# Fourier mixing and MLP on one core: the residual x added by accumulating DMAs, and the split of z done two quarters at a time

## The chip, the core and the metric

The kernel runs on one NeuronCore of one Trainium2 chip. A core has five engines that each follow a list of instructions in order: PE (matrix multiplication into PSUM), DVE (vector), ACT (scalar and activation functions), POOL (GpSimd) and SP. They wait for each other through semaphores. DMAs move data between DRAM and the on-chip memory SBUF; here SP and POOL issue nearly all of them, and each issue stands in its engine's list, in order, together with the wait in front of it. The metric is the device time of one execution in microseconds; the lower the better.

## The reference

With x of 2048 rows (the sequence) by 1024 columns (hidden), C and S the cosine and sine matrices of the discrete Fourier transform, and six rows `sa, ca, ga, sb, cb, gb` that are made from a conditioning vector `c`:

```python
h = _layernorm(x, axis=-1) * (1 + ca) + sa
a = jnp.einsum("bsd,ed->bse", h, dft_hid_re)
b = jnp.einsum("bsd,ed->bse", h, dft_hid_im)
y = jnp.einsum("ts,bse->bte", dft_seq_re, a) - jnp.einsum("ts,bse->bte", dft_seq_im, b)
x = x + ga * y
h = _layernorm(x, axis=-1) * (1 + cb) + sb
z = _layernorm(h, axis=-1)
x = x + gb * (gelu(z @ w1 + b1) @ w2 + b2)
```

All arrays are float32; w1 is 1024 x 3584 and w2 is 3584 x 1024. The change concerns the line `x = x + ga * y`, the mean in the layer norm behind it, and the preparation of `z` for the product with w1.

## The kernel before

The function `fast` computes everything under the assumption that the four Fourier matrices have the usual symmetries; it checks them on the way, and only if they don't hold does a second function, `general`, run. Only `fast` is changed.

**Stages.** First, up to about 215 us of the profile, x is loaded in 16 tiles of 128 rows, normalised (`ln1`, four tiles at a time), transposed, folded with the help of the symmetries, and transformed along the hidden dimension (`hid_unit`). Then comes the stage of the change, a loop over eight blocks `b` of two tiles each (L3171): `seq_tile` does the transform along the sequence for a tile (P and Q on PE) and evacuates it to SBUF as y with two DVE instructions (L3044, L3049); `ln2` forms x1 = x + ga * y, its layer norm with cb and sb, and the layer norm after that; `turn` transposes the result on PE and ACT copies it to a buffer `zt` (L3140); `z_tasks` splits it. Last come 28 groups of the product with w1 (`gemm3`, L3523) interleaved with 14 of the product with w2 (`gemm4`, L3632). The groups 0 to 12 of the first product use the first four blocks, which stay in SBUF; the z of blocks 4 to 7 is stored to DRAM by POOL (L3161) and loaded for the rest.

**The split of z.** The large products use seven products of half-size quarters in place of eight, and each float32 operand is a pair of float16 arrays, a high and a low part. `z_tasks` therefore takes the four quarters of a block (512 columns each), forms four differences on DVE in place (L2392, `comb`), and makes seven operands: the high part by ACT (L2367, `hi`) and the low part by DVE (L2377, `lo`).

**ln2 before.** For each tile n of a block: y = y * ga (L3104), y = y + x with the sum of each row kept (L3105), and a store of the tile, which is x1, to the output by POOL (L3107). x comes by `load_xw`, one DMA of 1 MB a block on SP's queue (L3066), into the block's work buffer `w`. Then: minus the mean (L3108), squares with their sum on ACT (L3088), (y - mean) * cb into w (L3113), a square root on ACT and a reciprocal refined on DVE (L2612 to L2621), times that and plus sb (L3117), the squares again with y as scratch (L3088), a second root, and the final scaling on ACT (L3126). Buffers y and w exist for three blocks.

**What sets the order.** Instructions are first collected as tasks with an engine, a cost, dependencies and a due time, in streams. A planner (`pick_first`, `fill_to`) takes the task of the least due time that can start at once, or the one that starts soonest, and thereby fixes each engine's list. Its clock is a model; it never sees the chip. The model counts a lag `LAT = 0.15` behind each dependency, 0.3 (`BEHIND`) ahead of a store, and a time to land:

```python
LANDS = {"dma": 2.0, "st": 4.0, ("st", "d"): 7.0, ("st", "u"): 5.0, ("st", "s"): 4.0, ("st", "z"): 4.0}
```

A task of kind "st" (made by `store`) is emitted, in POOL's or SP's list, as soon as the task that it depends on has been emitted. `flush` (L3391) ends this stage's planning; everything ahead of it precedes the first product on each engine. Behind it, POOL adds a row to the output by 16 DMAs that accumulate in DRAM (L3806), and later by others of that kind (L3730, L3705).

## Time and profile before

| | us |
|---|---|
| median of 3 runs | 1451.27 |
| lowest, highest run | 1444.45, 1453.93 |
| the execution that was profiled | 1453.19 |
| its span, first to last instruction | 1451.4 |
| first gated tile (L3104), start | 216.4 |
| last gated tile (L3104), start | 360.4 |
| time of one accumulating DMA's issue on POOL (L3806, median) | 0.868 |
| time of one plain store's issue on POOL (L3107, median) | 0.534 |

The profile is of one execution. Busy times of engines overlap; the mean duration of an instruction in a row is somewhat longer than the distance between two starts, because an engine begins the next instruction before the last one has drained. "x14" is a count; "out<-in" names the buffers, where `arena` is the one large SBUF buffer that nearly everything lives in, `ps` is PSUM, `fzc` the stored z, and `out_dram` the output. "idle ... <-X" is time in which the engine stood still until X released it. An engine name with q (SPq, POOLq) is its queue of issues and waits. A DMA's time to landing runs from its issue to its completion.

### The profile page before, as it was taken

How to read it: one execution, taken by the hardware profiler on the slowest of the kernel's cores; microseconds unless marked ns; L12 is line 12 of the kernel's file. 1: busy time of each engine (PE TensorE's matmuls, PEld its weight loads, DVE VectorE, ACT ScalarE, POOL GpSimd, SP SyncE). 2: the span in 40 equal slices, each digit the busy share in tenths (PEclk: the TensorE clock that was granted, in tenths of full speed). 3: DMA queues.
4: the chain of work that ended last, by engine and by line, in shares of the span. 5: the costliest groups of instructions: out<-in, count | busy, mean ns of one | idle time of the engine just before them, and what ended most of it. 6: DMA issues, size and time to landing. Idle time of an engine off the chain costs nothing.

```text
span 1451.4 us, 17321 instructions
## 1 busy us (share of the span) xinstructions
PE 1309.9 (90%) x6050; PEld 624.2 (43%) x6050; DVE 1105.7 (76%) x1668; ACT 749.5 (52%) x1209; POOL 260.3 (18%) x427
## 2 busy tenths in 40 slices
PE   5798979864487999999999999979999999999988
PEld 2344436543233444444444444434444444444433
DVE  5886738999657798989898898645666667777786
ACT  5486226787755683737373534145535353535340
POOL 3000000002420000000000000244443433353401
PEclk9798979986698999999999999999999999999999
DMA  9981442228698362626362539698877787876735
GB/s 371 369 317 45 131 130 102 87 103 292 226 202 272 115 226 95 225 95 225 109 225 95 202 111 368 178 323 278 294 247 233 249 292 244 288 249 241 233 125 119
DMA packets 108057, 302.29 MB, mean 208 GB/s; under 512 B 13836, under 2 KB 13852, under 8 KB 106040
## 3 DMA queue, kind: packets, MB, share of 16 engines
q1 hardware_dynamic: 74712, 192.49, 38.0%
q0 software_dynamic: 33216, 108.60, 23.7%
q8 instruction: 49, 0.80, 0.2%
q14 instruction: 48, 0.39, 0.1%
q10 hardware_dynamic: 32, 0.01, 0.0%
HBM read 216.10 MB, written 84.93 MB: 207 GB/s over the span
## 4 chain that ended last, share of the span: by engine, by line
PE 66%; issue 3%; DMA 2%; POOL 1%; DVE 1%; ACT 1%; POOLq 0%; ACTq 0%; DVEq 0%
PE ps L3632 35%; PE ps L3523 31%; DMA arena<-in_cre_dram 1%; DMA arena<-in_w_dram 1%; POOL fzc L3161 1%; DVE arena L2379 1%; POOL out_dram L3806 0%; ACT arena L2367 0%; POOL out_dram L3730 0%; DVE arena L2392 0%; POOL arena L3454 0%; DVE arena L3549 0%; ACT arena L3088 0%; ACT arena L3545 0%; ACT arena L3428 0%
## 5 line engine op out<-in xcount | busy, mean ns | idle before, releaser
L3523 PE MATMUL ps<-arena 128*128 128x512 f16 x2352 | 521.3, 384 | 25.5 <-ACT arena L3545 20.3
L3632 PE MATMUL ps<-arena 128*128 128x512 f16 x2352 | 512.6, 380 | 4.5 <-ACT arena L3668 4.5
L3523 PEld LDWEIGHTS <-arena 128*128 128x128 f16 x2352 | 232.5, 99 | 311.9 <-issue 41.3
L3632 PEld LDWEIGHTS <-arena 128*128 128x128 f16 x2352 | 230.8, 98 | 284.1 <-issue 8.1
L3678 DVE SCALAR_TENSOR_TENSOR arena<-ps,i4c,arena 128x1024 f32<-128x1024 f32 x179 | 229.4, 1282 | 99.9 <-PE ps L3632 96.7
L2392 DVE TENSOR_TENSOR arena<-arena 128x512 f32<-128x512 f32 (+1 forms) x228 | 171.4, 753 | 5.4 <-ACT arena L3140 1.1
L2367 ACT ACTIVATE arena<-arena,shc 128x512 f16<-128x512 f32 (+1 forms) x115 | 115.9, 1016 | 112.2 <-DVE arena L2392 62.6
L2379 DVE SCALAR_TENSOR_TENSOR arena<-arena,shc 128x512 f16<-128x512 f32 (+1 forms) x115 | 128.8, 1122 | 39.0 <-ACT arena L2367 38.8
L3428 ACT ACTIVATE arena<-arena 128x512 f32<-128x512 f32 (+5 forms) x148 | 91.1, 617 | 122.2 <-DVE arena L3437 119.0
L3542 ACT ACTIVATE arena<-arena,b1s,i1c 128x512 f32<-128x512 f32 x84 | 68.2, 814 | 118.8 <-DVE arena L3549 118.6
L3549 DVE TENSOR_TENSOR arena<-arena,ps 128x512 f32<-128x512 f32 x84 | 57.4, 685 | 61.1 <-PE ps L3523 60.5
L3437 DVE TENSOR_TENSOR arena<-arena 128x256 f32<-128x256 f32 x240 | 88.7, 419 | 16.9 <-DMA arena<-in_cre_dram 16.9
L2367 ACT ACTIVATE arena<-arena,s1c 128x512 f16<-128x512 f32 (+1 forms) x70 | 60.5, 886 | 71.2 <-DVE arena L2392 51.3
L3237 POOL PARTITION_ALL_REDUCE sums<-sums x21 | 12.7, 607 | 412.8 <-DVE sums L3233 408.1
L3454 POOL DMA_DIRECT2D arena<-in_cim_dram x99 | 53.6, 544 | 114.4 <-ACT arena L3428 105.2
L2379 DVE SCALAR_TENSOR_TENSOR arena<-arena,s1c 128x512 f16<-128x512 f32 (+1 forms) x70 | 66.3, 958 | 9.5 <-ACT arena L2367 9.4
L3545 ACT ACTIVATE arena<-ps 128x512 f32<-128x512 f32 x84 | 49.4, 589 | 38.8 <-PE ps L3523 38.8
L3454 POOL DMA_DIRECT2D arena<-in_cre_dram x99 | 54.2, 548 | 79.8 <-ACT arena L3428 62.7
L3225 ACT ACTIVATE ps<-arena 128x1024 f32<-128x1024 f32 x52 | 53.0, 1019 | 27.1 <-DMA arena<-in_w_dram 12.3
L2953 PE MATMUL ps<-arena 128*128 128x257 f16 (+5 forms) x297 | 54.2, 342 | 13.1 <-DVE arena L2518 8.3
L2885 PE MATMUL ps<-arena,scol 128*128 128x512 f32 x128 | 60.0, 618 | 3.4 <-DMA arena<-in_wm_dram 2.2
L2379 DVE SCALAR_TENSOR_TENSOR arena<-arena,s2c 128x1024 f16<-128x1024 f32 x49 | 61.9, 1279 | 1.4 <-ACT arena L2367 1.3
(198 smaller groups left out, 1217.6 us busy)
## 6 DMA issues: line engine op xcount, KB each, us to landing
fw<-arena SPq DMA_DIRECT2D x73, 512.0 KB, 5.7
arena<-fw SPq DMA_DIRECT2D x112, 256.0 KB, 4.7
arena<-fw SPq DMA_DIRECT2D x49, 512.0 KB, 4.6
arena<-in_cre_dram POOLq DMA_DIRECT2D x96, 256.0 KB, 4.7
arena<-in_cim_dram POOLq DMA_DIRECT2D x96, 256.0 KB, 5.2
out_dram<-arena POOLq DMA_DIRECT2D x44, 512.0 KB, 6.9
arena<-in_wm_dram SPq DMA_DIRECT2D x32, 512.0 KB, 7.3
arena<-in_w_dram SPq DMA_DIRECT2D x56, 256.0 KB, 3.7
```

The costliest lines, as they stand in the source:

```text
L2367: act.activation(o[m][0], q(j), AF.Copy, **sc)
L2379: dve.scalar_tensor_tensor(o[m][1], q(j), scale, o[m][0], op0=ALU.mult, op1=ALU.subtract)
L2392: dve.tensor_tensor(q(d), q(a), q(b), op=op)
L2885: pe.matmul(bank(6 + h), scol[:, k : k + 1].to_broadcast([P, P]), FA(o + 512 * h, (1, 512)), start=k == 0, stop=k == 7,)
L3428: f = lambda: act.activation(sq(a), sq(a), AF.Square, accum_out=csum[0:pn, n : n + 1])
L3437: dve.tensor_tensor(a[:, o::2], a[:, o::2], b[:, o::2], op=op)
L3454: return lambda t: gp.dma_start(t[0:pn], v)
L3523: pe.matmul(ps.rearrange("p (k t) -> p k t", k=4), w1c[:, m, s, a, d * P : (d + 1) * P], zc(m)[:, b, :, d, :], start=(start and d == 0 and ...
L3542: act.activation(dst, src, AF.Gelu_apprx_tanh, scale=inv, bias=b1s[:, 2 * p + j : 2 * p + j + 1])
L3549: after_pe("dve", 0.6, lambda: dve.tensor_tensor(q, q, ps[b], op=ALU.add), kp[b])
L3632: pe.matmul(t[:, j], hidc[:, c_, m, a, k * P : (k + 1) * P], w2c[:, m, c_, w], start=(start and c_ == 0 and n == 0), stop=(c_ == 1 and n = ...
L3678: lambda: dve.scalar_tensor_tensor(dst, ps[b], inv, dst, op0=ALU.mult, op1=ALU.add), kp[b],
```

## The change

- `load_xw` and its eight loads are removed. In `ln2` one DVE instruction per tile multiplies y by ga and keeps the sum of each row; then POOL issues a DMA that reads x from DRAM and adds it to y in SBUF (`accum_op=ALU.add`); the store of x1 waits for that DMA's landing, and so does the square of the tile (`("st", "xa", i)`). The squares, which write `w` first now, also take over the dependencies that `load_xw` had for the reuse of `w` (`wfree`).
- The sum no longer contains x. Its mean is kept from `ln1`: the small buffers `mvs` give way to columns of `csum`, which has an early use now, and where ACT makes the statistics (tiles 12 to 15) it scales so that the column is the mean itself. Minus the mean of x1 is then -sum/D minus the kept mean.
- `z_tasks` is written out instead of calling `right_tasks`. The high and the low parts take two quarters (1024 elements) in one instruction for the operands (0, 1), (3, 4), (2, 5), with 6 alone; of the differences the first two are one instruction, the others stay single. Each step has its dependencies written out.
- The planner counts no lag where a DVE or ACT task depends on one of its own engine (`by`). This holds for the whole of `fast`.

```diff
@@ class Task @@
-                    t = max(t, done.get(d, 1e12) + self.lag)
+                    t = max(t, done.get(d, 1e12) + (0.0 if by.get(d) == self.eng else self.lag))
...
         def run(self):
             t = self.start() + self.cost
+            if self.eng in ("dve", "act"):
+                by[self.key] = self.eng
@@ ln1 @@
-        mv, lc = mvs[bt % 2], lncs[bt % 2]
+        mv, lc = csum[:, 8 * bt : 8 * bt + 8].rearrange("p (q k) -> p q k", k=2), lncs[bt % 2]
...
-                act.activation(junk, FA(xr(i), (1, 1024)), AF.Copy, accum_out=mv[:, q, 0:1])
+                act.activation(junk, FA(xr(i), (1, 1024)), AF.Copy, scale=1.0 / D, accum_out=mv[:, q, 0:1])
...
-        scale, mean = (0.25, -1.0) if bt < ACT_STATS else (0.25 / D**3, -1.0 / D)
+        scale = 0.25 if bt < ACT_STATS else 0.25 / D
@@ ln2 @@
-    def load_xw(b):
-        f = lambda: sp.dma_start(wb(b), x_s[b // 4, 2 * b % 8 : 2 * b % 8 + 2].rearrange("r p e -> p r e"))
-        deps = [("turn", 2 * b - 6 + n) for n in range(2)] if b > 2 else [*copk, ("gbst", 0), ("gbst", 1)] if b > 1 else hops
-        load(("xw", b), f, deps, cost=2.8, stream="xw", due=70.0)
...
-        last[0] = ("xw", b)
+        wfree = [("turn", 2 * b - 6 + n) for n in range(2)] if b > 2 else [*copk, ("gbst", 0), ("gbst", 1)] if b > 1 else hops
         for n in range(2):
             i = 2 * b + n
-            step("dve", 1.23, lambda n=n: dve.tensor_tensor(y[:, n], y[:, n], ga_t, op=ALU.mult), [("y", i), *rows])
-            step("dve", 1.28, lambda n=n: dve.scalar_tensor_tensor(
-                y[:, n], y[:, n], 1.0, w[:, n], op0=ALU.mult, op1=ALU.add, accum_out=su[:, n : n + 1]), key=("x1", i))
-            store("x1", i, lambda n=n, i=i: gp.dma_start(o_s[i // 8, i % 8], y[:, n]), ("x1", i))
-        step("dve", 0.17, lambda: dve.tensor_scalar(nm, su, -1.0 / D, None, op0=ALU.mult))
+            last[0] = None
+            k = step("dve", 1.32, lambda n=n: dve.scalar_tensor_tensor(
+                y[:, n], y[:, n], 1.0, ga_t, op0=ALU.mult, op1=ALU.mult, accum_out=su[:, n : n + 1]), [("y", i), *rows])
+            store("xa", i, lambda n=n, i=i: gp.dma_start(y[:, n], x_s[i // 8, i % 8], accum_op=ALU.add), k)
+            store("x1", i, lambda n=n, i=i: gp.dma_start(o_s[i // 8, i % 8], y[:, n]), ("st", "xa", i))
+        step("dve", 0.17, lambda: dve.scalar_tensor_tensor(
+            nm, su, -1.0 / D, csum[:, 4 * b : 4 * b + 4 : 2], op0=ALU.mult, op1=ALU.subtract))
         q = sq(y, w, 1.0, nm)
         for n in range(2):
-            step("act", 1.35, q(n))
+            step("act", 1.35, q(n), [("st", "xa", 2 * b + n), *wfree])
@@ z_tasks @@
-        return right_tasks(
-            q, outs, None, 512, lambda j: ("zt", 2 * b + j % 2), lambda m: ("z", b, m), post=post if h else None,
-            free=(lambda m: slot("z", lambda: (b - 1, n[0]))) if h else None,
-        )
+        def hi(ms, js, deps):
+            def f():
...
+                act.activation(places(ms, 0), q(*js), AF.Copy)
...
+            add("z", "act", 0.17 + 0.44 * len(ms), f, deps + free, (b, "zhi", ms), due, f"z{b}")
+            return (b, "zhi", ms)
+
+        def lo(ms, js, deps):
+            def f():
+                dve.tensor_tensor(places(ms, 1), q(*js), places(ms, 0), op=ALU.subtract)
...
+            t = add("z", "dve", 0.13 + 0.54 * len(ms), f, deps, (b, "zlo", ms), due, f"z{b}")
+            return t
+
+        def comb(d, a, c, deps, key):
+            f = lambda: dve.tensor_tensor(q(*d), q(*a), q(*c), op=ALU.subtract)
+            return add("z", "dve", 0.15 + 0.54 * len(d), f, deps, (b, "zc", key), due, f"z{b}")
+
+        due = 110.0 + 22.0 * b
+        order = (0, 1, 3, 4, 2, 5, 6)
+        src = [("zt", 2 * b), ("zt", 2 * b + 1)]
+        k0 = lo((0, 1), (0, 2), [hi((0, 1), (0, 2), src[:1])])
+        k1 = comb((0, 1), (1, 3), (0, 1), [k0, *src], 0)
+        h1 = hi((3, 4), (0, 1), [k1])
+        k2 = lo((3, 4), (0, 1), [h1])
+        k3 = comb((1,), (3,), (0,), [k2], 1)
+        h2 = hi((2, 5), (1, 3), [k3])
+        k4 = comb((2,), (2,), (1,), [k3], 2)
+        k5 = lo((2, 5), (1, 3), [h2])
+        lo((6,), (2,), [hi((6,), (2,), [k4])])
@@ the loop over blocks @@
     for b in range(NB):
-        load_xw(b)
         for n in range(2):
             seq_tile(2 * b + n)
         ln2(b)
         for n in range(2):
             turn(2 * b + n)
-        push("z", f"z{b}", z_tasks(b), 110.0 + 22.0 * b)
+        z_tasks(b)
```

More of the change, by code (lines that the diff above doesn't have):

```diff
@@ L2598, in fast @@
     add("modm", "dve", 0.8, cols_out, ["cols", "max"], "mod", 1.0)
-    mvs = [mk([P, 4, 2], F32, f"mv{n}") for n in range(2)]
+    csum = mk([P, 160], F32, "csum")
     lncs = [mk([P, 4, 4], F32, f"lnc{n}") for n in range(2)]
@@ L3159, in post, with q @@
-        def post(m, o_):
-            dst = zc_d[m][:, :, k].rearrange("p a c t -> p a (c t)")
-            store("z", (b, at_[m]), lambda: gp.dma_start(dst, o_[2]), ("z", b, m), f"z{b}")
-        return right_tasks(
-            q, outs, None, 512, lambda j: ("zt", 2 * b + j % 2), lambda m: ("z", b, m), post=post if h else None,
-            free=(lambda m: slot("z", lambda: (b - 1, n[0]))) if h else None,
-        )
+        made = []
+        def q(i, j=None):
+            o = [ZT0 + 1024 * (n % 2) + 512 * (n // 2) for n in (i, i if j is None else j)]
+            return FA(o[0], (o[1] - o[0], 2), (1, 512)) if j is not None else FA(o[0], (1, 512))
@@ new lines, in places @@
+        def places(ms, a):
+            if h == 0:
+                o = [512 * O_ZC[m] + 2048 * a + 512 * k for m in ms]
+            else:
+                o = [512 * 184 + 256 + 1024 * made.index(m) + 512 * a for m in ms]
+            return HA(o[0], (o[1] - o[0], 2), (1, 512)) if len(ms) > 1 else HA(o[0], (1, 512))
+        def hi(ms, js, deps):
+            def f():
+                if h:
+                    for m in ms:
+                        if b > 4:
+                            reuse("z", (b - 1, len(made)))
+                        made.append(m)
+                act.activation(places(ms, 0), q(*js), AF.Copy)
+            n0 = order.index(ms[0])
+            free = [slot("z", (b - 1, n0 + i)) for i in range(len(ms))] if h else []
+            add("z", "act", 0.17 + 0.44 * len(ms), f, deps + free, (b, "zhi", ms), due, f"z{b}")
+            return (b, "zhi", ms)
```

26 lines of the change are left out of this document (10 added, 16 removed).

## The prediction

> **What bounds the kernel now.** I read the page first, for the stage that the change touches.
>
> ```profile
> span 1451.4 us, 17321 instructions
> ...
> PE   5798979864487999999999999979999999999988
> ...
> DVE  5886738999657798989898898645666667777786
> ...
> DMA  9981442228698362626362539698877787876735
> ...
> PE 66%; issue 3%; DMA 2%; POOL 1%; DVE 1%; ACT 1%; POOLq 0%; ACTq 0%; DVEq 0%
> ```
>
> A slice is 36.3 us. From slice 12 on PE is full: that is the two MLP matrix multiplications, which give PE its 66% of the chain of waits (the last line), and the diff leaves their instructions alone. In slices 7 to 9 (254 to 363 us) DVE stands at 9 while PE falls from 8 to 4: the sequence transform with the second layer norm and the splitting of z, which is all that the diff rewrites. I then cut that stretch and what follows it into windows (columns: PE, PEld, DVE, ACT and POOL busy with counts, granted clock, DMA share, GB/s), and grouped the DVE instructions of 226 to 365 us by line.
>
> ```profile
> 226.00:333.00 107.00, 85.77 (x542) 56.49 (x541) 103.42 (x188) 81.38 (x135) 6.03 (x11) 0.92 0.29 106
> 333.00:365.00 32.00, 10.23 (x48) 7.66 (x47) 31.17 (x60) 21.63 (x37) 9.73 (x15) 0.59 0.87 316
> 365.00:385.00 20.00, 5.98 (x25) 5.00 (x26) 14.89 (x30) 15.67 (x27) 4.78 (x7) 0.50 0.64 219
> 385.00:411.00 26.00, 18.35 (x73) 7.57 (x72) 9.99 (x31) 14.13 (x24) 12.51 (x18) 0.89 0.87 197
> 411.00:468.00 57.00, 48.17 (x206) 20.88 (x205) 40.48 (x52) 35.71 (x45) 8.66 (x11) 0.92 0.94 242
> ```
>
> ```profile
> L2377 DVE TENSOR_TENSOR arena<-arena 128x512 f16<-128x512 f32 x42 | 27.6, 684 | 0.0
> ...
> L3104 DVE TENSOR_TENSOR arena<-arena 128x1024 f32<-128x1024 f32 x14 | 17.1, 1222 | 0.2
> L3105 DVE SCALAR_TENSOR_TENSOR arena<-arena 128x1024 f32<-128x1024 f32 x14 | 17.1, 1220 | 0.2
> L2392 DVE TENSOR_TENSOR arena<-arena 128x512 f32<-128x512 f32 x24 | 16.5, 688 | 0.4
> ```
>
> DVE is busy 103.42 + 31.17 of 139 us, 97%; ACT 103.01, or 74%; no group of DVE waits for more than a fraction of a microsecond. So here a microsecond off DVE is a microsecond off the stage, as long as nothing new makes DVE wait. At 365 us that ends: a latency chain of the last block takes 20 us more, until PE starts the first MLP product. The timeline there, DVE, then ACT, then PE:
>
> ```profile
> 353.11 1.29 DVE L2377 TENSOR_TENSOR arena<-arena 128x512 f16<-128x512 f32 x2
> 354.32 1.41 DVE L2392 TENSOR_TENSOR arena<-arena 128x512 f32<-128x512 f32 x2
> 355.65 1.22 DVE L3105 SCALAR_TENSOR_TENSOR arena<-arena 128x1024 f32<-128x1024 f32 x1
> ...
> 359.66 0.68 DVE L3049 TENSOR_TENSOR arena<-ps,arena 128x512 f32<-128x512 f32 x1
> 360.38 1.23 DVE L3104 TENSOR_TENSOR arena<-arena 128x1024 f32<-128x1024 f32 x1
> 361.52 0.68 DVE L2392 TENSOR_TENSOR arena<-arena 128x512 f32<-128x512 f32 x1
> ...
> 362.73 1.22 DVE L3105 SCALAR_TENSOR_TENSOR arena<-arena 128x1024 f32<-128x1024 f32 x1
> ...
> 367.44 2.48 DVE L3113 SCALAR_TENSOR_TENSOR arena<-arena,lns 128x1024 f32<-128x1024 f32 x2 [2.20 <-ACT arena L3088]
> ```
>
> ```profile
> 366.17 1.14 ACT L3088 ACTIVATE arena<-arena,lns 128x1024 f32<-128x1024 f32 x1
> ...
> 367.31 1.14 ACT L3088 ACTIVATE arena<-arena,lns 128x1024 f32<-128x1024 f32 x1
> ```
>
> ```profile
> 382.96 1.97 PE L3136 MATMUL ps<-ident,arena 128*128 128x128 f32 x8 [2.73 <-ACT arena L3140]
> 384.72 6.33 PE L3523 MATMUL ps<-arena 128*128 128x512 f16 x24
> ```
>
> **The multiply that goes.** Today each of 16 tiles takes a multiply by ga (L3104) and an add of x (L3105). Afterwards one scalar_tensor_tensor multiplies and sums, with the shape of L3105, and the add is a DMA's. So L3104's slot is freed. From start to start a slot is 361.52 - 360.38 = 1.14 us; 14 of the 16 lie in the saturated stretch, so -16.0 us. The kept means replace one small instruction by another of the same kind: nothing.
>
> **z in pairs.** A low half of 512 takes 1.21 / 2 = 0.605 us from start to start (353.11 to 354.32), a combination 1.33 / 2 = 0.665 (354.32 to 355.65). Seven low halves become three of 1024, at L3104's 1.14, and one of 512: 4.24 against 4.03. Two of the four combinations become one: 1.33 against 1.14. That is 0.4 us a block, and the counts of 42 and 24 are six blocks: -2.4 us. Together DVE is relieved of 18.4 us. ACT, the next engine, would then be busy 103 us of some 120, 86%, so it isn't the bound.
>
> **The wait that comes.** The squares of a block (L3088) now wait until x has landed, and so does the store of x1, which stands right behind the accumulating DMA in POOL's queue: a store is emitted as soon as what it depends on has been. POOL therefore stands still from each issue to its landing, and behind it queue the z stores of blocks 4 to 7 and the next tile's accumulate. The trace has no accumulate into SBUF. The rows nearest to it are the plain store of a tile (whole run, then the four of the crowded window from 333 us), the accumulates into DRAM among other traffic (L3806) and the lone ones at the end (L3705), each with its time to landing; a last row follows for the queue.
>
> ```profile
> L3107 POOL DMA_DIRECT2D out_dram<-arena x16: 532/534/563, 219.3 to 364.4; - x16
> ...
> DMA to landing us min/median/max: 2.9/2.9/6.9
> ```
>
> ```profile
> L3107 POOL DMA_DIRECT2D out_dram<-arena x4: 554/560/563, 336.7 to 364.4; - x4
> ...
> DMA to landing us min/median/max: 3.1/4.2/6.9
> ```
>
> ```profile
> L3806 POOL DMA_DIRECT2D out_dram<-arena x16: 853/868/937, 395.1 to 435.6; - x16
> ...
> DMA to landing us min/median/max: 5.6/8.7/13.0
> ```
>
> ```profile
> L3705 POOL DMA_DIRECT2D out_dram<-arena x4: 1197/1213/1376, 1414.8 to 1436.8; - x4
> ...
> DMA to landing us min/median/max: 6.0/6.0/6.2
> ```
>
> ```profile
> L3161 POOL DMA_DIRECT2D fzc<-arena x28: 667/678/831, 330.4 to 394.3; - x28
> ```
>
> The last row is POOL's other work there, the z stores. The others move 512 KB each. The bounds are 2.9 and 8.7; I take 5.0 in the quiet window (DMA share 0.29), nearer to the lone accumulate's 6.0 than to the plain 2.9, because its rows of 4 KB are half as many descriptors and its target is not DRAM. The planner orders the engines for a landing after 4.0. It also allows 0.45 from the instruction to the issue; on the chip that was 0.4 (the multiply-add ends at 363.95, its store is issued at 364.4). So x is 1.0 late for the planned next steps, the squares and L3113. Two things cover that: ACT's second square, planned at 1.35, takes 1.14, 0.2 less; and L3113's first half needs only the first square, as it shows by starting at 367.44, before the second ends at 368.45, so its 1.2 us of work lies over the rest. Cover 1.4, so blocks 1 to 5 wait for nothing (at 6.0: 0.6 each; at 2.9: still nothing). Block 0 meets DVE half idle while PE delivers its tiles: +1. In the crowded window the plain store took 4.2 against 2.9; 5.0 x 4.2 / 2.9 = 7.2, which is 1.8 us beyond the cover, for block 6: +2 (0 to 5).
>
> The Trainium skill speaks against the place of this DMA: "SBUF — State Buffer", section "Who interferes with whom", says that descriptor generation by GpSimd is starved while DVE runs in its two-port modes and advises moving such a DMA to a hardware queue, where this change does the reverse. This case's row disagrees so far: with DVE 97% busy the sixteen issues by POOL (L3107) took 0.532 to 0.563 us. By that rule the sum would lose up to one long DVE instruction per accumulate, which is a rival below. The same page of the Trainium skill, section "The DMA setup-cost knee (why "@ 1 MiB" ≠ asymptote)", fits a transfer at 2 us plus its bytes over 436 GB/s; an estimate from it is 3.2 us for a tile, near the plain row's 2.9 and without anything for the accumulate; by it neither block 6 nor the tail would wait longer and the sum would be some 5 us lower.
>
> **The load that leaves SP.** Eight loads of x go. Behind the last one SP's queue holds the weights of the first product:
>
> ```profile
> 327.31 0.37 SPq L3066 DMA_DIRECT2D arena<-in_x_dram  x1
> 333.32 17.71 SPq L3389 DMA_DIRECT2D arena<-fw  x14
> ```
>
> They start 6 us later, when block 5's buffers are free, so they follow the stage and not the load: 0.
>
> **The tail.** From the end of the last evacuation (360.34) to the end of the second square (368.45) it is 8.1 us, part of it z work of the block before. Afterwards: 1.3 for the multiply, 0.4, 7.2 to land, 1.15 for the second square, 0.2 of semaphores: 10.2, and up to 1.4 while POOL finishes two z stores (0.68 each) queued ahead of it. +3 (-2 to 6). The last block's z, no longer hidden under ln2, alternates between ACT and DVE in longer pieces; each pair makes the other engine wait for 1024 elements instead of 512, 0.5 us more on two steps of the chain: +1.
>
> **Sum.** -16.0 - 2.4 + 1 + 2 + 3 + 1 = -11.4. The profiled execution took 1453.2 us (span 1451.4), so 1441.8; the median of the runs is 1451.3, so I forecast 1440 there. What is late next is still DVE, at some 96%.
>
> **The rivals.**
> *Everything hides.* If a landing takes some 4 us even among the weights, block 6 and the tail add nothing: -18.4 + 1 + 1 = -16.4, so 1435. At the plain 2.9 the tail even shrinks: 1.3 + 0.4 + 2.9 + 1.15 + 0.2 = 6.0 for 8.1, so 1433; with block 0 and z at nothing too, 1431. For it: the target is SBUF and the plain stores are quick. Against it: the DMA share of 0.87.
>
> *The landing is late and POOL becomes the clock* (slower). Take L3806's 8.7 throughout. DVE then waits 8.7 + 0.4 - 4.45 - 1.4 = 3.25 in each of blocks 1 to 4: 13. In blocks 5 to 7 POOL's queue holds two accumulates with their stores, 2 x (8.7 + 0.55), and seven z stores at 0.68, 23.3 us, against 17.2 for a block (139 - 18.4 over the seven blocks of 14 tiles): 6 each, 18. Block 0 then adds 5, the tail 4.5, z's tail 1: -18.4 + 13 + 18 + 10.5 = +23, so 1474. The queue decides from 17.2 = 2 x (L + 0.55) + 4.8, a landing L of 5.7, upwards. For it: the lone accumulate already takes 6.0. Against it: that one has twice the descriptors and writes to DRAM.
>
> *DVE holds up POOL's issues.* If each accumulate's issue waits for one long DVE instruction, 1.2 us by L3105's row, 8 blocks x 1.2 = 10 of the gain go: 1450. The sixteen issues of L3107, none over 0.563 us, speak against it. It is what the Trainium skill's rule on the two-port modes, told above, would do here.
>
> *The gain is given back at the start of the first product.* PE is idle there 26 - 18.35 + 57 - 48.17 = 16.5 us with a DMA share of 0.87 to 0.94. Four accumulates now fall among the weights; L3806's 16 were issued in 40.5 us, 2.5 each, so up to 10 us more traffic, less the 20 x 0.36 = 7 that is free in 365 to 385. The planner also drops its lag between instructions of one engine, which reorders everything ahead of and beside the matrix products; its effect I bound by -3 and +5 from those same gaps. Together some +8: 1448. That the change doesn't do what it says I see no room for: the multiply leaves the list either way.
>
> **Chances and range.** Forecast (1436 to 1445) 0.42; all hidden (1430 to 1436) 0.20; descriptors starved 0.04; given back (1445 to 1455) 0.18; POOL the clock (1460 to 1480) 0.16. The likeliest is 1440. A range of 1429 to 1458 leaves out the last case and little else. What this measurement tells from no change is about 1%, 14.5 us: faster than 1436.8 takes the second case and three tenths of the first, 0.33; slower than 1465.8 most of the last, 0.13; between them 0.54.
>
> **What would show it.** In the changed profile L3104's line is gone; the average block falls from 139 / 7 = 19.9 us to about 17.5; the accumulate's row shows landing near 5 in the quiet window and 7 later; DVE has no wait for L3088 ahead of blocks 1 to 5 and some 2 us in block 6; POOL's wait ahead of the x1 stores is the landing; PE's first MLP product starts near 372 instead of 384.72, and PE's gaps after it are as before. I am wrong if landings exceed 6 us in the quiet window, if DVE's share falls below 90% there, or if the first product comes early and the end does not.

## The result and the profile after

| | before | after |
|---|---|---|
| median of 14 runs, us | 1446.84 | 1456.6 |
| lowest, highest run | 1441.42, 1456.29 | 1451.33, 1462.0 |
| ratio, 95% interval | | 1.0057 (1.0032 to 1.0083) |
| span of the profiled execution | 1451.4 | 1456.3 |

The kernel became 0.6% slower (8 us by the ratio, 10 by the medians), which is inside the 1% of the prediction's middle case and inside its range, but on the other side of the forecast of 1440. The page of the kernel after (busy tenths of PE, DVE and the DMA engines in 40 slices of 36.4 us):

```profile
span 1456.3 us, 17240 instructions
...
PE   5688796773487999999999999979999999999987
...
DVE  6887647886547798989898898655666767676785
...
DMA  9982523549799362626362539698877777876725
```

From slice 12 on PE looks as before. In slices 7 to 10, where DVE showed 9, 9, 9, 6 before, it now shows 8, 8, 6, 5. The windows of the prediction, again as PE, PEld, DVE, ACT and POOL busy (counts), granted clock, DMA share, GB/s:

```profile
226.00:333.00 107.00, 82.89 (x502) 55.15 (x503) 88.74 (x162) 82.02 (x124) 15.70 (x22) 0.86 0.47 112
333.00:365.00 32.00, 7.27 (x51) 5.46 (x49) 20.00 (x35) 14.23 (x22) 10.86 (x15) 0.63 0.96 293
365.00:385.00 20.00, 4.53 (x19) 3.33 (x17) 13.06 (x22) 13.36 (x21) 5.40 (x8) 0.50 0.76 214
```

DVE was busy 103.42 and 31.17 us in the first two; it is busy 88.74 (83%) and 20.00 (63%), and still the stage isn't over when it was: in 365 to 385 PE waits. The groups of DVE by line and form in 226 to 365 us (busy, mean ns | idle before them) say where it stood:

```profile
L3102 DVE SCALAR_TENSOR_TENSOR arena<-arena 128x1024 f32<-128x1024 f32 x13 | 15.9, 1221 | 0.1
L3112 DVE SCALAR_TENSOR_TENSOR arena<-arena,lns 128x1024 f32<-128x1024 f32 x12 | 15.2, 1282 | 19.3 <-ACT arena L3085 19.3
```

L3102 is the multiply with the row sum, alone now. L3112 is the former L3113, (x1 - mean) * cb; it waits for the square of its tile (L3085), and that for the landing of x. To compare stages I take the time from the first sequence product on PE (L3036, before L3034) to the first MLP product (L3555, before L3523). After:

```profile
198.37 2.76 PE L3036 MATMUL ps<-arena 128*128 128x512 f16 x12 [1.42 <-DVE arena L2520]
...
388.73 7.23 PE L3555 MATMUL ps<-arena 128*128 128x512 f16 x24
```

That is 190.4 us. In the first profile of before it was 209.33 to 384.72, 175.4, and in a second profile of before, taken beside the experiments (a span of 1440.6):

```profile
200.56 2.76 PE L3034 MATMUL ps<-arena 128*128 128x512 f16 x12 [1.42 <-DVE arena L2518]
...
376.43 6.54 PE L3523 MATMUL ps<-arena 128*128 128x512 f16 x24
```

175.9. The two agree to 0.5 us; differences of under 2 us between single profiles are taken for nothing here. So the stage became 15 us longer instead of 11 shorter. What follows it took 1066.7 and 1064.2 us before and 1067.6 after: 1 to 3 us came from there. Ahead of it 2 to 11 us were gained, which hides a part of the loss in the total. DVE's waits in the stage (200 to 395 us: total, times, longest):

```profile
DVE arena L3112 <- ACT arena L3085: 26.8, 8, 9.6
DVE arena L3046 <- PE ps L3024: 12.6, 5, 5.8
DVE arena L3173 <- ACT arena L3164: 9.3, 7, 2.2
```

and the starts of L3112 in blocks 1, 2, 4, 5 and 6 (in brackets the idle time before it):

```profile
235.71 1.28 DVE L3112 SCALAR_TENSOR_TENSOR arena<-arena,lns 128x1024 f32<-128x1024 f32 x1 [4.55 <-ACT arena L3085]
...
263.36 1.28 DVE L3112 SCALAR_TENSOR_TENSOR arena<-arena,lns 128x1024 f32<-128x1024 f32 x1 [3.50 <-ACT arena L3085]
...
299.98 2.47 DVE L3112 SCALAR_TENSOR_TENSOR arena<-arena,lns 128x1024 f32<-128x1024 f32 x2
317.76 2.48 DVE L3112 SCALAR_TENSOR_TENSOR arena<-arena,lns 128x1024 f32<-128x1024 f32 x2
...
353.01 1.28 DVE L3112 SCALAR_TENSOR_TENSOR arena<-arena,lns 128x1024 f32<-128x1024 f32 x1 [9.57 <-ACT arena L3085]
```

Before, the same wait came to 2.2 us in all. POOL's part of block 6 shows what the 9.57 us are made of:

```profile
335.76 0.56 POOL L3105 DMA_DIRECT2D out_dram<-arena  x1 [5.18 <-DMA arena<-in_x_dram]
...
336.33 2.13 POOL L3179 DMA_DIRECT2D fzc<-arena  x3
...
340.69 1.38 POOL L3179 DMA_DIRECT2D fzc<-arena  x2 [2.24 <-issue]
...
342.83 0.96 POOL L3104 DMA_DIRECT2D arena<-in_x_dram  x1 [0.76 <-DVE arena L3186]
...
352.06 0.56 POOL L3105 DMA_DIRECT2D out_dram<-arena  x1 [8.27 <-DMA arena<-in_x_dram]
```

Read it downwards. POOL stands still until the previous accumulate has landed, issues the store of that x1 (335.76), then five z stores that had queued behind it, with a pause of 2.24 us between them that the profile puts down to nothing ("issue"). The multiply of the next tile had started on DVE at 335.16 and took 1.23 us; its accumulate (L3104) goes out only at 342.83, and lands after 9.2 us, with the DMA engines 96% busy. Both a queue and a long landing are in this wait, and either could be the cause. A third possibility is that the engines' lists, made for a landing after 4.0 us, put the waiting instruction too early.

### The profile page after: what moved, and what is told of

It is laid out like the page before. It is cut to its first block, busy times and chain, and to the rows that moved or that the text cites. A ratio compares the mean times of both kernels' runs of the same rounds, so it can differ in the third digit from the quotient of the medians.

```text
span 1456.3 us, 17240 instructions
## 1 busy us (share of the span) xinstructions
PE 1299.8 (89%) x6050; PEld 620.9 (43%) x6050; DVE 1085.8 (75%) x1620; ACT 748.9 (51%) x1185; POOL 275.1 (19%) x443
## 4 chain that ended last, share of the span: by engine, by line
PE 70%; DMA 10%; issue 8%; DVE 6%; ACT 4%; POOL 2%; SPq 0%; POOLq 0%; DVEq 0%; ACTq 0%
PE ps L3664 33%; PE ps L3555 30%; DMA arena<-in_x_dram 4%; PE ps L2887 2%; DMA arena<-in_wm_dram 2%; DMA arena<-in_w_dram 2%; PE ps L2955 2%; DMA arena<-in_cre_dram 1%; DVE arena L2381 1%; DVE arena L3710 1%; DVE arena L3173 1%; ACT arena L2369 1%; PE ps L3024 0%; PE ps L3036 0%; PE ps L3135 0%
## 5 line engine op out<-in xcount | busy, mean ns | idle before, releaser
L3555 PE MATMUL ps<-arena 128*128 128x512 f16 x2352 | 522.0, 384 | 23.9 <-ACT arena L3577 19.0
L3555 PEld LDWEIGHTS <-arena 128*128 128x128 f16 x2352 | 232.9, 99 | 310.6 <-issue 40.4
L2394 DVE TENSOR_TENSOR arena<-arena 128x512 f32<-128x512 f32 (+1 forms) x196 | 149.6, 764 | 3.7
L3270 POOL PARTITION_ALL_REDUCE sums<-sums x21 | 12.8, 609 | 410.2 <-DVE sums L3266 405.5
L2887 PE MATMUL ps<-arena,scol 128*128 128x512 f32 x128 | 64.0, 650 | 13.2 <-DMA arena<-in_wm_dram 10.5
L3135 PE MATMUL ps<-ident,arena 128*128 128x128 f32 x128 | 22.5, 333 | 56.0 <-ACT arena L3125 47.9
L3024 PE MATMUL ps<-arena 128*128 128x256 f16 (+3 forms) x400 | 53.9, 297 | 11.9 <-DVE arena L3051 11.9
```

Of the source, the lines that this page charges most:

```text
L2394: dve.tensor_tensor(q(d), q(a), q(b), op=op)
L2887: pe.matmul(bank(6 + h), scol[:, k : k + 1].to_broadcast([P, P]), FA(o + 512 * h, (1, 512)), start=k == 0, stop=k == 7,)
L3555: pe.matmul(ps.rearrange("p (k t) -> p k t", k=4), w1c[:, m, s, a, d * P : (d + 1) * P], zc(m)[:, b, :, d, :], start=(start and d == 0 and ...
```

## The experiments

My theory after this was that POOL's queue costs the time: the store of x1 waits in it for the landing, and everything behind it stands. The rivals were the landing itself against the planned 4.0 us, the planner's new rule without lag, and the pairs of z. All kernels ran beside the kernel before; the ratios are against its runs in the same set (medians of 1447.7 to 1448.5 in the sets of the experiments), and the stage is from one profile of each.

| kernel | median, us | ratio (95%) | stage, us | DVE's wait L3112 <- L3085 |
|---|---|---|---|---|
| before | 1446.84 | | 175.4, 175.9 | 2.2 |
| after | 1456.6 | 1.0057 (1.0032 to 1.0083) | 190.4 | 26.8 |
| 1 x1 stored by SP | 1448.02 | 1.0002 (0.9978 to 1.0026) | 183.5 | 19.9 |
| 2 x1 stored behind the squares | 1451.1 | 1.0018 (0.9997 to 1.004) | 184.7 | 18.0 |
| 3 after, z as before | 1459.96 | 1.008 (1.0055 to 1.0106) | 195.9 | 34.0 |
| 4 before, planner without lag | 1446.54 | 0.9974 (0.9954 to 0.9995) | 181.9 | |
| 5 before, z in pairs | 1442.36 | 0.9986 (0.9963 to 1.0009) | 171.8 | |
| 6 after, planner with lag | 1453.34 | 1.0038 (1.0014 to 1.0063) | 178.0 | 3.7 |
| 7 x1 by SP, landing planned at 6.2 | 1434.0 | 0.991 (0.9882 to 0.9939) | 166.5 | 4.3 |
| 8 after, landing planned at 6.2 | 1448.1 | 0.9999 (0.9976 to 1.0022) | 180.7 | 9.5 |
| 9 x lands over the gated rows | 1449.54 | 1.0003 (0.9982 to 1.0023) | 180.4 | 17.2 |
| 10 before, no lag and pairs | 1443.16 | 0.9975 (0.9955 to 0.9994) | 177.6 | |
| 11 before with the DMAs alone | 1457.85 | 1.0087 (1.005 to 1.0125) | 187.3 | 25.0 |

**0. The kernel before once more**, for a second profile; it is the one shown above, in one run of 1442.4 us.

> The kernel before, unchanged, for a second profile. The first profile has the sequence stage's first product at 209.3 us, the changed kernel and three kernels of the first set have it between 195 and 198, the kernel before with the planner's lag among them. Theory (the planner's lag starts the stage earlier): 209 again within 3 us. Rival (the first profile had a slower clock ahead of the stage, 0.73 between 160 and 200 us): near 198, and the changed kernel then gains nothing ahead of the stage.

Its stage is that of the first profile, and its start isn't: how long the stage takes can be compared between single profiles, when it starts only roughly.

**1. The store of x1 on SP's queue.** Nothing else changes; PE, DVE and ACT keep their lists instruction for instruction.

```diff
-            store("x1", i, lambda n=n, i=i: gp.dma_start(o_s[i // 8, i % 8], y[:, n]), ("st", "xa", i))
+            store("x1", i, lambda n=n, i=i: sp.dma_start(o_s[i // 8, i % 8], y[:, n]), ("st", "xa", i))
```

> The changed kernel with one edit: the store of x1 is issued by SP instead of POOL, so POOL no longer stands behind each accumulate until it lands. PE's, DVE's and ACT's lists are the same instruction for instruction; only POOL's and SP's differ. Theory (POOL's queue): the accumulates then go out some 0.4 us after their multiply, DVE's waits for the squares (L3112, 19.3 us between 226 and 365) fall to about 8, the first MLP product starts near 376 instead of 388.7, and the kernel is 9 to 13 us faster than the changed one, about 1444. Rival (the landing alone): the accumulate's own 6 us against the planned 4 make the waits; then the waits stay above 15 and the time moves by less than 3 us. Second rival (SP's queue): the stores hold up the weights behind them on SP, and the start of the first product loses what the stage gains.

The stage fell by 6.9 us and the time by some 8. DVE's waits in it:

```profile
DVE arena L3112 <- ACT arena L3085: 19.9, 8, 4.7
```

The longest one halved, and it is another: the 9.6 of block 6 became 2.9, the 4.7 is block 1's. So nearly all of the 6.9 us came from block 6, and most of the total stayed, where waits of about 8 us had been expected. Two things changed in block 6. The accumulate went out 3.0 us after the end of its multiply in place of 6.4, which is the queue. And from that issue to the start of the square that it releases it took 5.7 us in place of 8.9. The shorter landing goes with something else that the edit did. The loads of the first product's weights stand behind the stores in SP's queue, and they began 146.0 us after the stage's first product in place of 125.9, so that the DMAs moved 191 GB/s between that issue and that square in place of 322:

```profile
341.45 1.75 SPq L3422 DMA_DIRECT2D arena<-fw  x3
```

This run does not separate the two. That the later weights give the gain back, the rival of this experiment, did not come: the rest of the span is 1068.8 us against 1067.6. With each accumulate alone in front of its wait, the time from its issue to the start of the square was 5.8 to 7.0 us in three quiet places.

**2. The store of x1 behind the square, on POOL.** The store is emitted after the square of its tile has been, so that a next accumulate may precede it.

```diff
-            store("x1", i, lambda n=n, i=i: gp.dma_start(o_s[i // 8, i % 8], y[:, n]), ("st", "xa", i))
...
-            step("act", 1.35, q(n), [("st", "xa", 2 * b + n), *wfree])
+            i = 2 * b + n
+            k = step("act", 1.35, q(n), [("st", "xa", i), *wfree])
+            store("x1", i, lambda n=n, i=i: gp.dma_start(o_s[i // 8, i % 8], y[:, n]), k)
```

> The changed kernel with the store of x1 still on POOL but emitted behind the tile's first square instead of right behind its accumulate. Theory (POOL's queue): the next accumulate and the z stores pass ahead of it, so about the same gain as with the store on SP, 8 to 12 us against the changed kernel. Rival (the landing alone): less than 3 us. If this gains and the store on SP does not, SP's queue is what matters there.

5.7 us less of stage and 5.5 of time, where 8 to 12 had been expected. Here the weights start as in the kernel after (123.4 us after the first product) and the lists of PE, DVE and ACT are again the same, so this gain is the order of POOL's queue. It does not lie where experiment 1 had it: block 6 still waits 6.9 us, and block 7's 5.0 became 1.2.

**3. The kernel after with z as before.** `z_tasks` and its call are those of the kernel before.

```diff
-        z_tasks(b)
+        push("z", f"z{b}", z_tasks(b), 110.0 + 22.0 * b)
```

> The changed kernel with the old splitting of z (one quarter an instruction). Theory (POOL's queue): the pairs save 0.4 us of DVE a block, but DVE has idle time now, so undoing them moves the time by -2 to +4. Rival (the pairs lengthen the chain between ACT and DVE and cost more than they save): 4 us or more faster than the changed kernel, the waits of L3173 on L3164 gone.

The stage is 5.5 us longer than after: the pairs gain, and aren't the cause.

**4. The planner's rule alone**, in the kernel before.

```diff
-    done = {}
+    done, by = {}, {}
...
-                    t = max(t, done.get(d, 1e12) + self.lag)
+                    t = max(t, done.get(d, 1e12) + (0.0 if by.get(d) == self.eng else self.lag))
...
+            if self.eng in ("dve", "act"):
+                by[self.key] = self.eng
```

> The kernel before with one part of the change: no lag in the planner between instructions of one engine. The changed kernel's first product of the sequence stage starts 11 us earlier (198.4 against 209.3). Theory: that came from the loads of x leaving SP's queue, so here the stage starts within 3 us of 209.3 and the time is within 4 us of before. Rival: it came from the planner's order, so here the stage starts near 198 and the kernel is some 10 us faster than before.

The stage begins earlier, at 195.21 us, and is some 6 us longer; the time is the same to 0.3% (lower, with an interval that just leaves out no change). I had put the earlier start down to the loads that leave SP's queue; here they are all there and it comes nevertheless, so that reading falls. All nine profiles without the lag start the stage at 194.1 to 198.4, all five with it at 200.6 to 209.3.

**5. The pairs of z alone**, in the kernel before.

```diff
-        push("z", f"z{b}", z_tasks(b), 110.0 + 22.0 * b)
+        z_tasks(b)
```

> The kernel before with one part of the change: z split in pairs, x still loaded by SP and added by DVE. Where DVE is full the saving of 0.4 us a block should show: theory, 1 to 4 us faster than before, the median about 1446. Rival (the longer pieces make ACT and DVE wait for one another): 2 us or more slower.

171.8 for some 175.6: 3.8 us of stage. The interval of the time, 0.9963 to 1.0009, holds that and also nothing.

**6. The kernel after with the planner's lag.**

```diff
-                    t = max(t, done.get(d, 1e12) + (0.0 if by.get(d) == self.eng else self.lag))
+                    t = max(t, done.get(d, 1e12) + self.lag)
```

> The changed kernel with the planner's lag put back. The lag alone made the kernel before 0.26% faster, so if the parts add up this one is 2 to 6 us slower than the changed kernel, 1459 to 1462. Rival (the lag left DVE slack that covered part of the late landing): the same or faster than the changed kernel, 1452 to 1457, with less than 27 us of waits of L3112 on the squares.

It came out 3 us faster than after (the intervals overlap), as the rival of this experiment had it, with a stage of 178.0, 12 shorter, but a later start (208.2). The waits of DVE, and one of ACT, in its stage:

```profile
DVE arena L3173 <- ACT arena L3164: 23.3, 11, 7.6
DVE arena L3112 <- ACT arena L3085: 3.7, 2, 2.7
...
ACT arena L3164 <- DMA fzc<-arena: 5.4, 2, 4.6
```

With another order of the same instructions L3112 hardly waits. The wait has moved to the z split: its low halves (L3173) wait for the high ones (L3164), and twice those wait for the landing of a z store, by POOL, that frees their buffer.

**7. The store on SP and the landing planned.** One line to experiment 1: the planner is told a landing after 6.2 us, about what the traces show, in place of the 4.0 that it uses for stores.

```diff
-    LANDS = {"dma": 2.0, "st": 4.0, ("st", "d"): 7.0, ("st", "u"): 5.0, ("st", "s"): 4.0, ("st", "z"): 4.0}
+    LANDS = {"dma": 2.0, "st": 4.0, ("st", "d"): 7.0, ("st", "u"): 5.0, ("st", "s"): 4.0, ("st", "z"): 4.0, ("st", "xa"): 6.2}
```

> The changed kernel with the store of x1 on SP and the planner told that an accumulate lands after 6.2 us, not 4.0. With the store on SP, DVE still waited 19.9 us for the squares. Theory (what is left is an order made for too early a landing): the waits fall below 8 us, the stage shortens by 8 to 12 us more, and the kernel is faster than before, 1436 to 1441. Rival (the block's longer chain itself is short of work to put under it, whatever the order): DVE's idle time only moves to other lines, and the time stays within 4 us of the one with the store on SP, 1448.

It took 1434.0, 0.9% less than before. Its window from 226 to 333 us, its wait and the two ends of its stage:

```profile
226.00:333.00 107.00, 78.34 (x520) 53.20 (x518) 99.40 (x180) 87.13 (x134) 15.50 (x19) 0.88 0.55 133
```

```profile
DVE arena L3112 <- ACT arena L3085: 4.3, 2, 2.7
```

```profile
197.31 2.76 PE L3036 MATMUL ps<-arena 128*128 128x512 f16 x12 [1.42 <-DVE arena L2520]
...
363.83 6.18 PE L3555 MATMUL ps<-arena 128*128 128x512 f16 x24
```

DVE is at 99.40 of 107, 93%, L3112 waits 4.3 us instead of 26.8, and the stage is 166.5 us, 23.9 less than after. What the change takes from DVE now shows in the time.

**8. The landing planned, the store on POOL.** The same line of `LANDS`, in the kernel after.

> The changed kernel, x1 stored by POOL as in the change, with the planner told that an accumulate lands after 6.2 us. Theory (two causes, each worth some 8 to 12 us: POOL standing behind each accumulate, and an order made for a landing at 4.0): the waits of L3112 on the squares fall from 26.8 to below 12 and the time is 6 to 12 us below the changed kernel, 1445 to 1450, and well above the 1434 of both edits. Rival (the planned landing is all of it, and the store on SP mattered only through it): within 4 us of 1434. Rival (POOL's queue is all of it): within 3 us of the changed kernel.

With experiments 1 and 7 this gives a square, of the stage in us:

| landing in the planner | x1 stored by POOL | by SP |
|---|---|---|
| 4.0 | 190.4 | 183.5 |
| 6.2 | 180.7 | 166.5 |

In each row PE, DVE and ACT have the same lists, instruction for instruction; only SP's and POOL's differ. Planning alone is worth 9.7, the store's move alone 6.9, both 23.9: more than the sum of 16.6. In the right column the weights also start later than in the left one (146.0 against 125.9 us after the first product in the first row, 134.0 against 123.8 in the second), so what it gains is the store's move together with that, and no run parts them. With either fault left in place a part of the other's gain is waited away; here it is at the z split, as in experiment 6:

```profile
DVE arena L3173 <- ACT arena L3164: 13.4, 9, 6.6
...
DVE arena L3112 <- ACT arena L3085: 9.5, 3, 4.9
```

**9. The same transfer without the addition.** The engines' lists stay those of the kernel after; x overwrites the gated rows.

```diff
-            store("xa", i, lambda n=n, i=i: gp.dma_start(y[:, n], x_s[i // 8, i % 8], accum_op=ALU.add), k)
+            store("xa", i, lambda n=n, i=i: gp.dma_start(y[:, n], x_s[i // 8, i % 8]), k)
```

> The changed kernel with a plain DMA in place of the accumulating one: x overwrites the gated rows and the gated transform is left out of x1. Everything else, the waits and POOL's queue among them, stays. Theory (the accumulate's landing is what is long): POOL's wait ahead of each x1 store falls from some 5.3 to about 2.5 us, as a plain store lands after 2.9; the planned 4.0 then covers it, the waits of L3112 fall below 8 and the time is 10 to 18 us below the changed kernel, 1439 to 1446. Rival (any DMA on POOL with a wait behind it does the same): landings within 1 us of the accumulate's and the time within 4 us of the changed kernel.

The issues of L3104 (duration min/median/max) here, and a quiet landing, seen between the DMA's issue and the store that waits for it:

```profile
L3104 POOL DMA_DIRECT2D arena<-in_x_dram x16: 533/534/800, 205.1 to 351.7; - x16
```

```profile
250.90 0.53 POOL L3104 DMA_DIRECT2D arena<-in_x_dram  x1 [1.34 <-DVE lns L3106]
255.19 0.53 POOL L3105 DMA_DIRECT2D out_dram<-arena  x1 [3.75 <-DMA arena<-in_x_dram]
```

and in the kernel after:

```profile
L3104 POOL DMA_DIRECT2D arena<-in_x_dram x16: 866/873/1212, 207.1 to 363.2; - x16
```

```profile
256.02 0.87 POOL L3104 DMA_DIRECT2D arena<-in_x_dram  x1
...
262.40 0.55 POOL L3105 DMA_DIRECT2D out_dram<-arena  x1 [5.51 <-DMA arena<-in_x_dram]
```

From start to start 4.3 us against 6.4; of the thirteen quiet ones in each kernel the middle one is 4.3 (4.2 to 5.6) against 6.1. The landing is then near the 4.0 that the order was made for. The stage is 180.4, as short as with the order made for the true landing (180.7, experiment 8): two ways to bring plan and landing together, each worth 10 us. But the time fell by 7 us where 10 to 18 had been expected, and L3112 still waits 17.2 us where less than 8 had been. The waits of blocks 0, 2 and 3 fell from 7.3 us to 1.0; block 1's fell only from 4.9 to 4.4 and block 6's from 9.6 to 8.7. Block 1 shows why, on ACT and DVE:

```profile
229.07 1.02 ACT L3139 ACTIVATE arena<-ps 128x1024 f32<-128x1024 f32 x1 [0.93 <-PE ps L3135]
229.99 1.14 ACT L3085 ACTIVATE arena<-arena,lns 128x1024 f32<-128x1024 f32 x1
```

```profile
231.26 1.28 DVE L3112 SCALAR_TENSOR_TENSOR arena<-arena,lns 128x1024 f32<-128x1024 f32 x1 [4.06 <-ACT arena L3085]
```

The square (L3085) does not wait for x here; it stands in ACT's list behind a copy (L3139) that waits for PE. This wait is in the order, whatever the landing. In block 6 the DMA went out 5.9 us after the end of its multiply, behind five z stores, and landed 9.1 us later.

**10. The change without its DMAs**: the kernel before with the edits of experiments 4 and 5 together.

> The kernel before with the planner's lag removed and z in pairs, but x loaded by SP and added by DVE: the change without its DMAs. Alone the two gave 0.26% and 0.14%. Theory (they add): 4 to 8 us faster than before, the stage from its first product to the first MLP product some 4 us shorter than with the lag alone (181.9). Rival (they overlap in what they shorten): within 3 us of before.

The stage is 177.6 us, 4.3 shorter than with the planner's rule alone, as expected. The time is 0.25% below before, no more than with that rule alone (0.26%): the two don't add up in it.

**11. The DMAs without the rest**: the kernel after with the edits of experiments 3 and 6 together.

> The accumulating DMAs and kept means alone: the changed kernel with the planner's lag and the old splitting of z put back. With the lag and pairs the stage took 178 us from its first product, against 175.4 before; pairs alone took it to 171.8. If the parts add, this one takes some 182 us and is 6 to 10 us slower than before. Rival (the DMAs are neutral as the kernel before was planned, and only the lag turns them into a loss): within 3 us of before.

The time is 0.9% above before and the stage 187.3 us, more than the 6 to 10 us and the 182 expected. So the DMAs cost time in the order with the lag too, and the rival that they are neutral there is out.

With experiments 3 to 6 these two complete a table of the change's three parts (stage, us):

| planner, z | without the DMAs | with them | difference |
|---|---|---|---|
| lag, single quarters | 175.6 | 187.3 | +11.7 |
| lag, pairs | 171.8 | 178.0 | +6.2 |
| no lag, single quarters | 181.9 | 195.9 | +14.0 |
| no lag, pairs | 177.6 | 190.4 | +12.8 |

(175.6 is the mean of the two profiles.) The DMAs lengthen the stage in every row, the pairs shorten it with either rule of the planner, by 3.8 and 4.3 without the DMAs and by 9.3 and 5.5 with them. Done as in experiment 7, the same DMAs shorten the last row's 177.6 to 166.5.

## Why the prediction was wrong

**The step that failed** is the one under "the wait that comes": "I take 5.0 in the quiet window", and from it "Cover 1.4, so blocks 1 to 5 wait for nothing". In the kernel after the quiet landings, from the issue to the store that waits for them, were 5.9 to 7.5 us (thirteen of them, the middle one 6.1), those of the crowded window 7.6 to 9.2. Experiment 7's trace has the landing itself, without the wait behind it, over all sixteen:

```profile
L3104 POOL DMA_DIRECT2D arena<-in_x_dram x16: 851/866/938, 206.1 to 336.9; - x16
...
DMA to landing us min/median/max: 5.5/5.8/8.6
```

The nearest row of the trace before, the lone accumulate of L3705 at 6.0, was right; I moved it down for the shorter descriptor list and the target in SBUF, and no row bore that out. A row of the trace before even spoke against it: the plain loads of x into SBUF, of twice the bytes, took 5.5 us where the plain store of a tile took 2.9.

```profile
L3066 SPq DMA_DIRECT2D arena<-in_x_dram x8: 368/368/432, 168.4 to 327.3; - x8
...
DMA to landing us min/median/max: 5.4/5.5/6.1
```

Blocks 4 and 5 indeed waited for nothing; blocks 1 to 3 waited 4.9, 3.5 and 1.3, block 0 2.5 and block 6 9.6. Together 21.8, where the forecast had +1 and +2. In the stage the forecast's -11.4 and the measured +14.8 lie 26 us apart; 19 of them are these waits, 1 the tail, and the planner's rule, some 6 on the kernel before, is of the size of the rest. Experiment 7 closes the account from the other side: 22.5 us less of this wait, 23.9 less of stage.

**My own allowance was too coarse, too.** At 6.0 the working gave 0.6 a block, so the landing alone does not make the 21.8. The working reckoned one landing against one gap of the planner, and forgot what it had said a few lines earlier, that z stores and the next tile's accumulate queue behind the store that waits. In block 6 the issue came 6.4 us after its multiply (which ends at 336.4; the issue is at 342.83), where the working had 0.4. And it took the order for free of waits as long as x lands on time. Experiment 9, with landings near the planned 4.0 in the quiet window, still has 14.2 of the 21.8 us in these blocks: 4.4 in block 1, from the order itself, 1.0 in block 2, and 8.7 in block 6, from the queue and the crowded landing.

**The rival that came** is "the landing is late and POOL becomes the clock", at 0.16. Its own threshold, a landing of 5.7, was below the row of 6.0 that I had in hand, and should have had far more of the chance. Its mechanism, POOL's queue, is shown by experiment 2 at 5.7 us; its size, +23, was for 8.7 throughout. It was also only a part of the loss: the lists planned for 4.0, which I used as a number in the cover and never as a cause, are another, 9.7 us by themselves (experiment 8).

**DVE's relief**, -16.0 and -2.4, was real. DVE's busy time over the span fell from 1105.7 to 1085.8 us, 19.9, and experiment 7 turned it into time: 11.1 us of stage against experiment 10.

**The pairs of z** were sized at -2.4 with +1 in the tail; the profiles give 3.8 to 5.5 in three pairings and 9.3 in one, the tail included.

**The tail** was priced at 10.2 us from the last evacuation's end to the second square's end. It was 12.2 (359.9 to 372.1). The square waited for its x:

```profile
370.96 1.15 ACT L3085 ACTIVATE arena<-arena,lns 128x1024 f32<-128x1024 f32 x1 [3.68 <-DMA arena<-in_x_dram]
```

Its accumulate was issued at 363.18, so 7.8 us, near the 7.2 assumed. The issue came 2.0 us after the multiply's end, behind the previous tile's store and two z stores, where the sum had 0.4 and a possible 1.4 more.

**The load that leaves SP**, taken as 0, was nothing:

```profile
324.25 17.59 SPq L3422 DMA_DIRECT2D arena<-fw  x14
```

The weights start 125.9 us after the stage's first product; before it was 124.0 (333.32 less 209.33). They follow the stage.

**DVE holding up POOL's issues** (0.04) did not show in the quiet window. The issues there took 0.87 to 0.92 us, the same as the accumulates into DRAM before. The Trainium skill's rule from "SBUF — State Buffer", section "Who interferes with whom", on starved descriptor generation, is for DVE's two-port modes, and the same section says that tensor_tensor has none. DVE's long instructions in this stage are tensor_tensor and scalar_tensor_tensor, so the rows of this case do not speak against the rule, as the prediction had it, nor for it. In the crowded window the issues took 0.96 to 1.21 us, and POOL paused between z stores (2.24 us in block 6); what made either is not shown.

**The gain given back at the start of the first product** did not come from traffic: the rest of the span is 1067.6 us against 1064.2 and 1066.7, and in all profiles it goes with the planner's rule and not with the DMAs. It is 1063.2 to 1066.7 us in the five with the lag, two of which have the DMAs, and 1067.0 to 1071.1 in the nine without it, two of which don't have them. The planner's rule, bounded there by -3 and +5, was bounded too narrowly: ahead of the stage it gains 5 to 14 us on the kernel before (195.2 against 200.6 and 209.3) and 10 on the kernel after (198.4 against 208.2), within it it costs some 6 on the one and 12 on the other (178.0 to 190.4). In the total that about cancels: 0.9974 in experiment 4, and 3 us to its disadvantage in experiment 6, which the intervals there don't separate from nothing.

**What stays open** is why the stage is longer without the lag even where no DMA accumulates, and why the rest of the span is. No experiment takes the two orders apart. What makes the stage's start earlier is shown in part. With the lag, PE stands 8.3 to 11.7 us in all five profiles ahead of the last 81 products before the stage, until DVE releases them; in the nine without it this wait is 0.6 us at most, and PE's longest wait there is 6.2 to 7.1 us for a load (L2887). These products in the kernel before, its second profile and the kernel after:

```profile
190.66 17.25 PE L2953 MATMUL ps<-arena 128*128 128x257 f16 x81 [8.33 <-DVE arena L2518]
```

```profile
186.67 12.47 PE L2953 MATMUL ps<-arena 128*128 128x257 f16 x81 [11.73 <-DVE arena L2518]
```

```profile
185.36 11.59 PE L2955 MATMUL ps<-arena 128*128 128x257 f16 x81
```

They took 17.25 and 12.47 us in the two profiles of one kernel. The windows from 160 to 200 us of the kernel before, its second profile and the kernel after differ in the granted clock (the third number from the end):

```profile
160.00:200.00 40.00, 29.47 (x114) 13.46 (x113) 23.32 (x23) 12.48 (x13) 1.23 (x4) 0.73 0.69 214
```

```profile
160.00:200.00 40.00, 26.17 (x147) 14.05 (x146) 22.61 (x24) 11.98 (x15) 1.23 (x4) 0.83 0.65 198
```

```profile
160.00:200.00 40.00, 30.52 (x160) 15.85 (x159) 20.11 (x23) 10.59 (x14) 1.23 (x4) 0.87 0.46 140
```

0.73 and 0.83 with the lag, 0.87 without. The clock thus differs between two profiles of one kernel too, and these products are the quicker the higher it is. Whether the order changes the clock was not tried.

## What to carry to other kernels

When an instruction of the busiest engine is replaced by a DMA, take its landing from the nearest row of the same kind without a discount, and give that landing to whatever orders the engines: the same change cost 8 to 10 us here with an order made for 4 us, and gained 13 with one made for 6.2 and the waiting store moved. An instruction that waits for a landing must not stand in the queue that issues the next such DMA. A freed engine is a gain only as far as its later waits don't grow; sum those waits by line before and after, and look at them before the total.

## What the runs showed of the hardware

- An accumulating DMA of 512 KB from DRAM into SBUF, issued by POOL, took 0.87 us to issue and 5.9 to 7.5 us until the instruction that waited for it began, the middle one 6.1; in the crowded window from 333 us (DMA share 0.96, then 0.76) 0.96 to 1.21 and 7.6 to 9.2. The same transfer without the addition took 0.53 us and 4.2 to 5.6, the middle one 4.3 (5.9 to 9.1 in the crowded window). The addition is thus some 2 us.
- A wait for one DMA ahead of a dependent one is what the Trainium skill advises ("DMA: Bandwidth & Descriptors", section "Two DMAs through the same engine are not ordered": the issuing engine waits on the first one's semaphore). The row of POOL's waits in the kernel after shows its price when that engine has other DMAs to issue:

```profile
POOL out_dram L3105 <- DMA arena<-in_x_dram: 88.1, 15, 8.3
```

With the store behind the tile's square in the same queue the stage was 5.7 us shorter; with the wait in SP's queue, and the weights later behind it, 6.9 to 14.2.
